# The opening of a two-stage Fourier and MLP kernel in another order: weight rounding, the first weight products, one row turned on TensorE, and the loads

## The chip, the cores and the metric

The kernel runs on one core of a Trainium2 chip. A core has five engines with queues of their own: TensorE (PE, and PEld for its weight loads), VectorE (DVE), ScalarE (ACT), GpSimd (POOL) and SyncE (SP), which only issues transfers here; 16 DMA engines carry them out. An engine takes its instructions in the order in which they were written, and waits at one whose inputs or buffers are not ready. The metric is the device time of one execution in microseconds (us); the median of several runs counts.

## What is computed

```python
def _attn_setup():
    batch, seq, dim = (8, 3008, 256)
...
def _attn_ref(x) -> np.ndarray:
    X = np.fft.fft(x, axis=1)
    X = np.fft.fft(X, axis=2)
    return X.real.astype(np.float32)
...
def _moe_ref(x, w_in, w_out) -> np.ndarray:
    h = x @ w_in
    g = h * (1.0 / (1.0 + np.exp(-1.702 * h)))
    return (g @ w_out).astype(np.float32)
```

The real part of a two-dimensional Fourier transform of each of 8 batches (3008 x 256) goes, row by row, through a layer of width 2048 with a GELU. `x` is float32; the two weight matrices arrive as 64-bit words (`w_in` 256 x 2048, `w_out` 2048 x 256) and are float32 in value after rounding.

## The kernel before

**Stages.** The transform along the sequence has a first stage of length 47 and a second of length 64; the transform along the 256 columns is folded into `w_in`. The first stage (`fold1`, `mix1`; for the first batch `fold_first`, `mix_first`) leaves its result in `xt`. `spill` writes it to a buffer in device memory (`Td`), `fill` reads it back turned (`t4`, 12 blocks). `rotate` rewrites one column of `t4` by a product, and `stage2` makes a tile `pq` from four blocks: 64 small products into two PSUM banks, and four VectorE transposes out of them (L320), two for each bank.

**The main loop** (L669) has 8 batches x 3 blocks x 2 halves x 8 pairs of feature groups: 384 steps and 3 to drain. Step t does `hidden(t)` (TensorE products `pa` and `pb` with the folded weights `wcs`, L448, and a ScalarE copy `v`, L452), `product(t - 3)` (products with `wo`, L515), `activate(t - 1)` (GELU, L477), sums on GpSimd and VectorE, and `rows(t)` on VectorE: L462, then `dif` (L465), which needs the row `nb` and a column of `af2`, then L472. Whatever else belongs to a step hangs in `extra[t]` and is issued at its end, in the order in which it was put there; `early` names the steps at which `fold_w` runs.

**Weights.** Each matrix comes in four chunks (in0 to in3, out0 to out3), 1 MB each, into three buffers `raw`. A chunk goes through
- `bounds`: the square `g` of the high words (ScalarE L359, for in0 VectorE L357), `m`, the high words held within bounds (GpSimd L360), and `r`, the low words as rounding bits, by two ScalarE activations (L362, L363);
- `rounded`: three VectorE instructions, L373 (`m` from `g` and `m`), L375 and L376 (`a` from `m`);
- `finish`: GpSimd adds `a` and `r` (L380), into `wst` for an in-chunk and in two halves into `wo` for an out-chunk.

There is one buffer for `m` and one for `a`, so `m` of a chunk waits for L376 of the chunk before, and L375 of a chunk waits for the chunk before's L380. There are two buffers for `r`.

`fold_w(n)` multiplies `wst[n]` by the column transform (`psw`, L418), copies both halves to `wcs` on ScalarE (L420), and makes a row on one partition (L424). A transfer (L425) turns that row into four columns of `af2`. `hidden(0)` and `hidden(1)` need chunk 0, `hidden(2)` and `hidden(3)` chunk 1, and so on.

**The opening.** Four rounds k of `fold_first` and `mix_first` work on x as it arrives. Each ends in ScalarE copies, of one column in the middle (L248) and into `xt` at the end (L264), and from k = 1 on in a spill, by SP's queue and partly by ScalarE's. The spill of k = 3 goes in two pieces, with the fill of the first four blocks between them. Then come `load_out(0)`, the rounding of in0, five warm-up products (L278), the bounds of in1, `fold_w(0)`, the fill's rest, `load_out(1)`, `rotate`, `stage2`, the rounding of in1, the bounds of out0 and `load_in(2)`. `nyquist(0, 0)` in step 0 makes the row `nb` by a product (`psn`, L331) and a ScalarE copy (L332).

**Buffers that set the order.** Four PSUM banks serve all of `psw`, `psr`, `ps2`, `psn`, `pa` and `pb`: a product that starts a new tile waits until one of the four is read out. All transfers on SP's queue are issued in order; one that waits for its buffer, or for a spill to land, holds those behind it.

Of the kernel before, what the change touches and what calls it, by code (L numbers as in the profile page):

```python
# [27 lines left out]
F32 = mybir.dt.float32  # L28
U32 = mybir.dt.uint32
ALU = mybir.AluOpType  # L30
ACTF = mybir.ActivationFunctionType
# [8 lines left out]
NU, NG = 2, 12  # L40
# [10 lines left out]
def free(ap, offset, *dims):  # L51
    return bass.AP(ap.tensor, ap.offset + offset, [list(ap.ap[0])] + [list(d) for d in dims])
# [57 lines left out]
def kernel(ctx: ExitStack, tc, x, w_in, w_out, tab1, tab2, out):  # L110
    nc = tc.nc
# [14 lines left out]
    cv = ctx.enter_context(tc.tile_pool(name="cv", bufs=1, space=SB))  # L126
# [16 lines left out]
    af2 = const.tile([128, NF], F32, tag="af2", name="af2")  # L143
    ones = const.tile([1, 128], F32, tag="ones", name="ones")
# [5 lines left out]
    def bank(name):  # L150
        return psm.tile([128, 512], F32, tag="mm", name=name)
# [122 lines left out]
    def warm(n):  # L274

        ps = bank("warm")
        for _ in range(n):
            nc.tensor.matmul(ps[:], lhsT=wcs[0][:, 0:128], rhs=wcs[0][:, 0:512], start=True, stop=True)  # L278
# [13 lines left out]
    def fill(b, a0=0, a1=NG):  # L292
        if a0 == 0:
            t4t[b] = tp.tile([128, NG, D], F32, tag="t4", name="t4")
        nc.sync.dma_start(out=t4t[b][:, a0:a1, :], in_=Td[b].rearrange("(a p) d -> p a d", p=128)[:, a0:a1, :])

    def rotate(b, a0=0, a1=NG, copy=None):

        col = t4t[b][:, a0:a1, H]
        ps = bank("psr")  # L300
        nc.tensor.matmul(ps[:, 0:a1 - a0], lhsT=rot, rhs=col, start=True, stop=True)
        (copy or nc.vector.tensor_copy)(col, ps[:, 0:a1 - a0])

    def stage2(b, blk):

        pq, t4 = pqp.tile([128, 2, 512], F32, tag="pq", name="pq"), t4t[b]
        pqt[b, blk] = pq
        ps = [bank("ps2") for _ in range(NU)]
        for cs in range(2):
            for h in range(2):  # L310
                for g in range(4):
                    for u in range(NU):
                        rows, at = slice(64 * u, 64 * u + 64), cs * 256 + h * 128
                        nc.tensor.matmul(ps[u][32 * g:32 * g + 32, at:at + 128], lhsT=m2[rows, cs, h * RUN:(h + 1) * RUN],  # L314
                                         rhs=t4[rows, 4 * blk:4 * blk + 4, cs * H + 32 * g:cs * H + 32 * g + 32],
                                         start=True, stop=True)
        for u in range(NU):
            for cs in range(2):

                nc.vector.transpose(free(pq[:], cs * 512 + u * RUN, [256, 2], [NU * RUN, 4], [1, RUN]),  # L320
                                    free(ps[u][:], cs * 256, [128, 2], [32, 4], [1, 32]))
# [13 lines left out]
    raw = {}  # L335

    def load_in(n, eng):
        t = raw["in", n] = cv.tile([128, 1024, 2], U32, tag="raw", bufs=3, name="raw")
        eng.dma_start(out=t[:].rearrange("p (i f) w -> p i (f w)", i=2),
                      in_=w_in[:, n * 512:(n + 1) * 512].bitcast(U32).rearrange("(i p) f -> p i f", p=128))  # L340

    def load_out(n, eng):
        t = raw["out", n] = cv.tile([128, 1024, 2], U32, tag="raw", bufs=3, name="raw")
        eng.dma_start(out=t[:].rearrange("p (f n) w -> p f (n w)", f=4),
                      in_=w_out[4 * n * 128:(4 * n + 4) * 128, :].bitcast(U32).rearrange("(p f) n -> p f n", p=128))

    pre = {}

    def bounds(key, first=False):


        hi, lo = raw[key][:, :, 1].bitcast(F32), raw[key][:, :, 0]
        g = sp.tile([128, 1024], F32, tag="s", bufs=3, name="g")
        m = cv.tile([128, 1024], F32, tag="m", name="m")
        r = cv.tile([128, 1024], U32, tag="r", bufs=2, name="r")
        if first:
            nc.vector.tensor_tensor(g[:], hi, hi, op=ALU.mult)  # L357
        else:
            nc.scalar.activation(g[:], hi, ACTF.Square)  # L359
        nc.gpsimd.tensor_scalar(m[:], hi, scalar1=TOP, scalar2=-TOP, op0=ALU.min, op1=ALU.max)  # L360

        nc.scalar.activation(r[:].bitcast(F32), lo, ACTF.Copy, scale=2.0 ** -29, bias=2.0 ** 23)  # L362
        nc.scalar.activation(r[:], r[:].bitcast(F32), ACTF.Copy, bias=-2.0 ** 23)  # L363
        pre[key] = g, m, r

    def rounded(outs, key):

# [19 lines left out]
    def round_in(n):  # L387
        wst[n] = op.tile([128, 2, 512], F32, tag="os", name="wst")
        out = wst[n][:].rearrange("p i f -> p (i f)")
        last["in", n] = rounded(lambda *ins: [(out, ins)], ("in", n))  # L390
# [10 lines left out]
    def finish_in(n):  # L401
        last["in", n]()
# [11 lines left out]
    def fold_w(n):  # L414
        for cs in range(2):
            ps = bank("psw")
            for i in range(2):
                nc.tensor.matmul(ps[:], lhsT=cd[:, i, cs, :], rhs=wst[n][:, i, :], start=(i == 0), stop=(i == 1))  # L418

            nc.scalar.copy(wcs[cs][:, n * 512:(n + 1) * 512].rearrange("p (f c) -> p f c", f=4),  # L420
                           free(ps[:], 0, [1, 4], [4, 128]))

        row = cv.tile([1, 512], F32, tag="e", name="row")
        nc.scalar.activation(row[:], ps[0:1, :], ACTF.Copy, scale=2.0)  # L424
        nc.scalar.dma_start(out=af2[:, 4 * n:4 * n + 4], in_=row[:])  # L425


    NP = NF // 2
# [153 lines left out]
    first = tp.tile([128, NG, D], F32, tag="t4", name="first")  # L582
# [16 lines left out]
    for k, need in enumerate(((0, 7, 1), (6, 2), (5, 3), (4,))):  # L599
# [3 lines left out]
        if k:  # L603

            for m in ((0, NM),) if k < 3 else ((0, 16), (16, NM)):
                spill(0, ((0, 2), (2, 1), (3, 1))[k - 1], (nc.sync, nc.scalar if k > 1 else nc.sync), *m)
                if k == 3 and m[0] == 0:
                    fill(0, 0, 4)
    load_out(0, nc.sync)
    bounds(("in", 0), True)  # L610
    round_in(0)
    finish_in(0)
    warm(5)
    bounds(("in", 1))
    fold_w(0)
    fill(0, 4, NG)
    load_out(1, nc.sync)
    rotate(0, 0, 4, nc.scalar.copy)
    stage2(0, 0)
    round_in(1)  # L620
    finish_in(1)
    bounds(("out", 0))
    load_in(2, nc.sync)

    extra, early = {}, {}

    def at(t, fn, *args):
        extra.setdefault(t, []).append((fn, args))

    n = len(steps)  # L630

    ahead = [("out", 0), ("in", 2), ("out", 1), ("in", 3), ("out", 2), ("out", 3)]
    for t, (kind, c) in enumerate(ahead):
# [1 line left out]
        if t + 1 < len(ahead):  # L635
            at(t, bounds, ahead[t + 1])
        at(t + 1, finish_out if kind == "out" else finish_in, c)
    early[1], early[3], early[5] = 1, 2, 3
    for t, load, c in ((0, load_in, 3), (1, load_out, 2), (2, load_out, 3)):
        at(t, load, c, nc.sync)  # L640
    at(3, load_matrices)
    if B > 1:
# [5 lines left out]
    for b in range(B):  # L648
        t0 = b * NBLK * NF
        late = 0 if b else 3  # L650
        if b + 2 < B:
            at(t0 + 10, turn, b + 2)
        if b + 1 < B:
            for c in range(NCH):
                at(t0 + 7 + 2 * c + late, fold1, b + 1, c, nc.gpsimd)
                if c % 2:
                    at(t0 + 8 + 2 * c + late, mix1, b + 1, c // 2)
            at(t0 + 24 + late, spill, b + 1)
            at(t0 + 29 + late, fill, b + 1)
            if b + 2 < B:  # L660
                at(t0 + 33 + late, load_x, b + 2)
            at(t0 + 36 + late, rotate, b + 1)
        for blk in range(NBLK):
            nxt = (b, blk + 1) if blk + 1 < NBLK else (b + 1, 0)
            if nxt[0] < B:
                at(t0 + blk * NF + 8, stage2, *nxt)
                at(t0 + blk * NF + 12, nyquist, *nxt)

    for t in range(n + LAG):  # L669
        if t < n:  # L670
            hidden(t)
        if t == 0:
            nyquist(0, 0)
        if t >= LAG:
            product(t - LAG)
        if t in early:
            fold_w(early[t])

        if 0 < t <= n:
            activate(t - 1)  # L680
            sums(t - 1, nc.gpsimd)
        sums(t - 2, nc.vector)
        if t < n:
            rows(t)
        if t >= LAG:
            combine(t - LAG)
        for fn, args in extra.get(t, ()):
            fn(*args)
# [28 lines left out]
```

## Time and profile before

| | us |
|---|---|
| median of 4 runs | 1934.71 |
| lowest and highest of them | 1933.09 to 1935.99 |
| the profiled execution, its own time | 1932.98 |
| its span | 1931.0 |
| PE busy in the span | 1905.1 (99%) |
| DVE, ACT, POOL busy | 1408.1, 673.5, 764.6 |

The span runs from the first to the last instruction of the profiled execution; its time has 1.98 us more around it. Busy time counts an engine's instructions, without branches, waits and the issuing of transfers. A matmul in float32 is recorded as two passes, so a `psw` group of four matmuls is "x8". A wait's bracket, "[1.17 <-POOL wo L380]", names the idle time of the engine just before that row and whose instruction ended it. The chain that ended last is followed back from the last instruction; in it, "DMA raw" is time from the issue of a transfer to its landing.

### The profile page before, as it was taken

Reading aid. Unit: us, or ns where it says so; the run is one execution under the profiler, and the core shown is the slowest. Engines: PE = TensorE matmul, PEld = TensorE weight load, DVE = VectorE, ACT = ScalarE, POOL = GpSimd, SP = SyncE. Lnnn points to the kernel's source line nnn. Section 1 sums busy time; section 2 is a strip of 40 time slices with the busy share of each in tenths; the row PEclk is TensorE's granted clock in tenths of the full one; section 3 lists DMA queues with packets and bytes.
Section 4 is the critical chain, followed back from the end, with each engine's and each line's share of the span. In section 5 each row is a group of like instructions: output and inputs, shape, how many; then the busy total and the mean of one; then the engine's idle time right before and its main releaser. Section 6 shows DMA issues by size and latency. Waiting matters only on the chain.

```text
span 1931.0 us, 29514 instructions
## 1 busy us (share of the span) xinstructions
PE 1905.1 (99%) x10822; PEld 1667.1 (86%) x10822; DVE 1408.1 (73%) x2924; ACT 673.5 (35%) x928; POOL 764.6 (40%) x1061
## 2 busy tenths in 40 slices
PE   7899999999999999999999999999999999999998
PEld 4698888988889888888889888898888988889887
DVE  4777777876778767876777777777777777777766
ACT  4633333333333333333333333333333333333332
POOL 3665323542245322552235523364323642223222
PEclk9999999999999999999999999999999999999999
DMA  8730550227203452126322262221820223202201
GB/s 286 173 53 10 109 65 12 51 55 112 17 12 59 65 93 17 25 46 106 52 27 49 40 101 39 18 49 43 121 20 13 18 48 56 17 12 27 17 12 22
DMA packets 145552, 104.54 MB, mean 54 GB/s; under 512 B 105474, under 2 KB 128290, under 8 KB 143712
## 3 DMA queue, kind: packets, MB, share of 16 engines
q1 hardware_dynamic: 142976, 99.07, 30.4%
q0 software_dynamic: 384, 2.10, 0.4%
q8 instruction: 86, 1.41, 0.3%
q10 hardware_dynamic: 2048, 1.48, 0.3%
q14 instruction: 58, 0.48, 0.1%
HBM read 59.36 MB, written 48.01 MB: 56 GB/s over the span
## 4 chain that ended last, share of the span: by engine, by line
PE 96%; DMA 2%; ACT 1%; DVE 0%; POOL 0%; issue 0%; SPq 0%; ACTq 0%; DVEq 0%; POOLq 0%
PE po L515 59%; PE pa L448 17%; PE pb L448 17%; PE ps L210 1%; PE ps L314 1%; DMA xt<-in_x_dram 1%; DMA raw<-in_moe_w_in_dram 1%; PE psw L418 0%; DMA Td<-xt 0%; DMA af<-row 0%; PE ps L214 0%; POOL xt L229 0%; PE ps L259 0%; DVE e L237 0%; ACT g L359 0%
## 5 line engine op out<-in xcount | busy, mean ns | idle before, releaser
L489 POOL TENSOR_TENSOR s<-h 128x256 f32<-128x256 f32 (+1 forms) x376 | 270.3, 719 | 1093.6 <-ACT h L477 1028.0
L515 PE MATMUL po<-s,wt 128*128 128x256 f32 (+1 forms) x2256 | 599.7, 375 | 0.0
L452 ACT COPY v<-pa 128x512 f32<-128x512 f32 (+1 forms) x384 | 222.0, 578 | 1062.6 <-PE pa L448 1062.6
L462 DVE TENSOR_TENSOR h<-v,pb 128x512 f32<-128x512 f32 (+1 forms) x384 | 259.0, 674 | 402.8 <-PE pb L448 396.7
L515 PEld LDWEIGHTS po<-s,wt 128*128 128x128 f32 x2256 | 428.6, 190 | 48.4
L515 PE MATMUL po<-h,wo 128*128 128x256 f32 (+1 forms) x1632 | 469.7, 375 | 0.1
L477 ACT ACTIVATE h<-h 128x1024 f32<-128x1024 f32 (+1 forms) x384 | 400.8, 1044 | 18.2 <-DVE h L472 15.3
L448 PE MATMUL pa<-pq,wcs 128*128 128x256 f32 (+1 forms) x1536 | 393.8, 379 | 2.2 <-DVE pq L320 1.3
L448 PE MATMUL pb<-pq,wcs 128*128 128x256 f32 (+1 forms) x1536 | 387.9, 375 | 1.8 <-DVE dif L465 1.6
L515 PEld LDWEIGHTS po<-h,wo 128*128 128x128 f32 x1632 | 310.0, 190 | 36.0 <-issue 0.5
L448 PEld LDWEIGHTS pa<-pq,wcs 128*128 128x128 f32 x1536 | 286.8, 190 | 51.1 <-issue 11.9
L465 DVE SCALAR_TENSOR_TENSOR dif<-nb,af,pb 128x256 f32<-128x256 f32 (+1 forms) x768 | 328.2, 468 | 1.9 <-DMA af<-row 1.9
L448 PEld LDWEIGHTS pb<-pq,wcs 128*128 128x128 f32 x1536 | 291.5, 190 | 35.9 <-DVE dif L465 2.0
L490 POOL TENSOR_TENSOR s<-h 128x256 f32<-128x256 f32 (+1 forms) x376 | 276.7, 736 | 0.0
L472 DVE TENSOR_TENSOR h<-pa,dif 128x512 f32<-128x512 f32 (+1 forms) x448 | 265.4, 604 | 13.2
L515 PE MATMUL po<-h,wt 128*128 128x256 f32 (+1 forms) x752 | 220.3, 375 | 0.0
L515 PE MATMUL po<-s,wo 128*128 128x256 f32 (+1 forms) x752 | 220.3, 375 | 0.0
L493 DVE TENSOR_TENSOR s<-h,s 128x256 f32<-128x256 f32 (+1 forms) x376 | 204.0, 543 | 12.9
L492 DVE TENSOR_TENSOR s<-s,h 128x256 f32<-128x256 f32 (+1 forms) x376 | 178.8, 476 | 4.3 <-POOL s L489 4.3
L515 PEld LDWEIGHTS po<-h,wt 128*128 128x128 f32 x752 | 142.9, 190 | 16.1
L515 PEld LDWEIGHTS po<-s,wo 128*128 128x128 f32 x752 | 142.9, 190 | 16.1
L196 POOL TENSOR_TENSOR xt<-xt 111x510 f32<-111x510 f32 x56 | 73.8, 1318 | 4.4
(67 smaller groups left out, 699.8 us busy)
## 6 DMA issues: line engine op xcount, KB each, us to landing
out_dram<-os SPq DMA_DIRECT2D x284, 64.0 KB
Td<-xt SPq DMA_DIRECT2D x14, 768.0 KB
t<-Td SPq DMA_DIRECT2D x7, 1536.0 KB
xt<-in_x_dram SPq DMA_DIRECT2D x14, 512.0 KB
xt<-Xr SPq DMA_DIRECT2D x14, 512.0 KB
nb<-pq SPq DMA_DIRECT2D x23, 256.0 KB
out_dram<-os SPq DMA_DIRECT2D x96, 56.0 KB
Xr<-in_x_dram SPq DMA_DIRECT2D x7, 752.0 KB
```

The costliest lines, as they stand in the source:

```text
L196: eng.tensor_tensor(low, low, free(t, up + D - 1, [-D, 2], [-1, D - 1]), op=ALU.add)
L448: nc.tensor.matmul(ps[:, i * 256:i * 256 + n], lhsT=wcs[cs][:, f * 128:(f + 1) * 128], rhs=pq[:, cs, ks], start=True, stop=True)
L452: nc.scalar.copy(two(v[:], n), two(pa[:], n))
L462: nc.vector.tensor_tensor(two(h[:], n), two(v[:], n), two(pb[:], n), op=ALU.add)
L465: nc.vector.scalar_tensor_tensor(dif[:, i * 256:i * 256 + n], nb[:, ks], af2[:, f:f + 1], pb[:, i * 256:i * 256 + n], op0=ALU.mult, op1=AL ...
L472: nc.vector.tensor_tensor(free(h[:], 512 + at + m - 1, [256, 2], [RUN, blocks], [-1, m]), *ins, op=ALU.add)
L477: nc.scalar.activation(g, g, ACTF.Gelu_apprx_sigmoid)
L489: eng.tensor_tensor(s1, a21, a22, op=ALU.add)
L490: eng.tensor_tensor(s3, a11, a21, op=ALU.subtract)
L492: eng.tensor_tensor(s2, s1, a11, op=ALU.subtract)
L493: eng.tensor_tensor(s4, a12, s2, op=ALU.subtract)
L515: nc.tensor.matmul(pot[q][:, i, :n], lhsT=lhs, rhs=rhs, start=(p == 0 and i == 0 and f == 0), stop=(p == NP - 1), skip_group_check=True)
```

## The change

- `stage2` issues the four transposes in another order: first the `cs = 0` half of both banks, then the `cs = 1` half.
- The two activations that make `r` are a function `low_bits`. For in0 they run in the opening right after round k = 1, and `bounds` takes their result; for the other chunks they run inside `bounds` as before.
- `fold_w(0)` turns its row into the columns of `af2` by four products (L424's row as weights, one column of ones), and a ScalarE copy; the other three chunks keep the transfer.
- In the opening, `load_in(2)` follows `load_out(0)`; in1 is rounded and finished ahead of `fold_w(0)`; four warm-up products, not five, stand after that; the copy in `rotate` is VectorE's and not ScalarE's.
- `fold_w(1)` moves from step 1 to step 0. `load_out(1)` moves to step 0, the fill's rest and `load_in(3)` to step 1, `load_out(2)` and `load_out(3)` to steps 2 and 3.

```diff
-        for u in range(NU):
-            for cs in range(2):
+        for cs in range(2):
+            for u in range(NU):
 
                 nc.vector.transpose(free(pq[:], cs * 512 + u * RUN, [256, 2], [NU * RUN, 4], [1, RUN]),
                                     free(ps[u][:], cs * 256, [128, 2], [32, 4], [1, 32]))
...
-    def bounds(key, first=False):
-
-
-        hi, lo = raw[key][:, :, 1].bitcast(F32), raw[key][:, :, 0]
+    def low_bits(key):
+        r = cv.tile([128, 1024], U32, tag="r", bufs=2, name="r")
+
+        nc.scalar.activation(r[:].bitcast(F32), raw[key][:, :, 0], ACTF.Copy, scale=2.0 ** -29, bias=2.0 ** 23)
+        nc.scalar.activation(r[:], r[:].bitcast(F32), ACTF.Copy, bias=-2.0 ** 23)
+        return r
+
+    def bounds(key, r=None):
+
+
+        hi = raw[key][:, :, 1].bitcast(F32)
         g = sp.tile([128, 1024], F32, tag="s", bufs=3, name="g")
         m = cv.tile([128, 1024], F32, tag="m", name="m")
-        r = cv.tile([128, 1024], U32, tag="r", bufs=2, name="r")
-        if first:
+        if r:
             nc.vector.tensor_tensor(g[:], hi, hi, op=ALU.mult)
         else:
             nc.scalar.activation(g[:], hi, ACTF.Square)
         nc.gpsimd.tensor_scalar(m[:], hi, scalar1=TOP, scalar2=-TOP, op0=ALU.min, op1=ALU.max)
-
-        nc.scalar.activation(r[:].bitcast(F32), lo, ACTF.Copy, scale=2.0 ** -29, bias=2.0 ** 23)
-        nc.scalar.activation(r[:], r[:].bitcast(F32), ACTF.Copy, bias=-2.0 ** 23)
-        pre[key] = g, m, r
+        pre[key] = g, m, r or low_bits(key)
...
-        nc.scalar.dma_start(out=af2[:, 4 * n:4 * n + 4], in_=row[:])
+        if n:
+            nc.scalar.dma_start(out=af2[:, 4 * n:4 * n + 4], in_=row[:])
+            return
+        ps = bank("psf")
+        for f in range(4):
+            nc.tensor.matmul(ps[:, f:f + 1], lhsT=free(row[:], f, [4, 128]), rhs=ones[:, 0:1], start=True, stop=True)
+        nc.scalar.copy(af2[:, 0:4], ps[:, 0:4])
...
                 if k == 3 and m[0] == 0:
                     fill(0, 0, 4)
-    load_out(0, nc.sync)
-    bounds(("in", 0), True)
+        if k == 1:
+            r0 = low_bits(("in", 0))
+    for load, c in ((load_out, 0), (load_in, 2)):
+        load(c, nc.sync)
+    bounds(("in", 0), r0)
     round_in(0)
     finish_in(0)
-    warm(5)
     bounds(("in", 1))
-    fold_w(0)
-    fill(0, 4, NG)
-    load_out(1, nc.sync)
-    rotate(0, 0, 4, nc.scalar.copy)
-    stage2(0, 0)
     round_in(1)
     finish_in(1)
+    warm(4)
+    fold_w(0)
+    rotate(0, 0, 4)
+    stage2(0, 0)
     bounds(("out", 0))
-    load_in(2, nc.sync)
...
-    early[1], early[3], early[5] = 1, 2, 3
-    for t, load, c in ((0, load_in, 3), (1, load_out, 2), (2, load_out, 3)):
+    early[0], early[3], early[5] = 1, 2, 3
+    at(0, load_out, 1, nc.sync)
+    at(1, fill, 0, 4, NG)
+    for t, load, c in ((1, load_in, 3), (2, load_out, 2), (3, load_out, 3)):
         at(t, load, c, nc.sync)
```

## The prediction

> **What bounds the kernel now.** I first read the windows view in three stretches, then the waits and the chain of waits of the opening, then the timeline row by row. The columns of a windows row are start:end, length, then the busy time and count of PE, PEld, DVE, ACT and POOL, then PE clock, DMA share and GB/s.
>
> ```profile
> 0.00:80.00 80.00, 60.72 (x460) 37.47 (x461) 45.11 (x63) 46.04 (x64) 33.98 (x35) 0.94 0.81 252
> 80.00:1900.00 1820.00, 1820.00 (x10252) 1608.49 (x10251) 1347.03 (x2830) 621.37 (x858) 724.07 (x1017) 1.00 0.30 46
> 1900.00:1931.00 31.00, 24.41 (x114) 21.14 (x112) 16.01 (x33) 6.06 (x8) 6.58 (x10) 0.97 0.08 18
> ```
>
> From 80 to 1900 us TensorE is never idle. The change adds almost no TensorE work there and takes none away, so its whole effect is the moment at which TensorE becomes continuously busy. Before 80 it stands still for 19.28 us in all, and much of that is the wait for x. So I follow only the opening, and ask when product 2 starts (79.01 in the chain below), after which TensorE has no gap.
>
> ```profile
> POOL wst L380 <- DVE a L376: 10.1, 1, 10.1
> POOL wst L380 <- ACT r L363: 8.4, 1, 8.4
> ACT g L359 <- DMA raw<-in_moe_w_in_dram: 2.8, 1, 2.8
> ```
>
> These waits (us, times, longest) are the ones that the change goes for: chunk in0 waits for ScalarE's low bits, chunk in1 for VectorE, and ScalarE's Square for the late load of chunk in2. The chain of waits (start, length) shows which of them reach the end:
>
> ```profile
> 33.27 4.03 DMA Td<-xt
> ...
> 38.46 11.52 DMA raw<-in_moe_w_in_dram
> ...
> 50.06 1.15 ACT g L359
> ...
> 64.10 5.41 PE psw L418 x8
> ...
> 70.63 6.30 DMA af<-row
> 76.95 0.88 DVE dif L465 x2
> ...
> 79.01 3.45 PE po L515 x16
> 82.46 3.43 PE psw L418 x8
> ```
>
> The load of in2 sits in SP's queue behind a fill that waits for the spill, lands at 50.02 and sends ScalarE late into its work. The timeline gives the rest; the bracket is the idle time before a row and what ended it:
>
> ```profile
> 33.54 2.36 POOL L380 TENSOR_TENSOR wst<-a,r 128x1024 uint32<-128x1024 uint32 x1 [8.40 <-ACT r L363]
> 42.41 1.44 DVE L320 STREAM_TRANSPOSE pq<-ps 128x256 f32<-128x256 f32 x4 [11.67 <-PE ps L314]
> 45.50 0.29 PEld L331 LDWEIGHTS psn<-pq,ones 1*128 1x128 f32 x2 [0.33 <-issue]
> 58.50 0.69 DVE L375 TENSOR_SCALAR a<-m 128x1024 uint32<-128x1024 uint32 x1 [1.17 <-POOL wo L380]
> 66.00:68.00 2.00, 2.00 (x3) 0.67 (x2) 1.97 (x3) 1.30 (x3) 0.66 (x1) 0.50 1.15 211
> ```
>
> The fourth row shows a second limit: VectorE's rounding of a chunk waits until GpSimd has added the chunk before. The last (a windows row again) is a TensorE clock of half for some 4 us, of which more below.
>
> **The change, step by step.** Durations are rows of this trace.
>
> *Low bits of in0 early.* ScalarE ends its copies of k=1 at 24.43 and next ran at 24.98. Two activations (31.23 to 33.46, 2.23 us) now come in between, so the L248 copies of k=2 start at 26.66: 1.68 later, and with them the second half of mix_first 2, all of k=3 and the spills that ScalarE's own queue issues. TensorE ends mix_first 3 at 30.9 (29.2), the last xt copy ends at 32.0 (30.31), fill 0:4 is issued at 34.55 (32.85). In return the GpSimd add of in0 waits only for VectorE (29.52+1.23): 30.8 to 33.15, where it ended at 35.90.
>
> *Warm 4, then fold_w(0).* Four warm products are 8 passes of 0.43, 3.44 us: 30.9 to 34.3. That covers the wait until 33.15; without them fold_w(0) would start 1.1 earlier. It runs 34.3 to 37.75 instead of 35.95 to 39.4: a gain of 1.65.
>
> *The row by products.* Before, copies and row ended 1.35 after psw (40.75), then an issue of 0.56, and the rotation's copy stood behind it on ScalarE (41.44). Now the row ends at 39.1 and four products, 8 passes, follow on TensorE, with rotate and stage 2 queued behind them. No row shows a product of one column. From below: the two weight loads of the psn row, 0.18 each, take 0.29 together, so they start 0.11 apart; 8 x 0.11 = 0.9. From above: a pass of the main products, 3.45/16 = 0.215, so 1.7. The operands are nearest to psn's (one row), so I take 1.0: 40.15. Rotation 0.35, its copy on an idle VectorE under stage 2's first half, two halves of 0.67 each: 41.85. The transposes start at 41.95; in the new order pa needs two (0.36 each) and not three: pa 0 at 42.75 (43.58), a gain of 0.83. The 1.65 is half lost, to the round trip row, TensorE. In the later 23 blocks the transposed tile is read 8 steps on, so the order is worth nothing there. The row's transfer, which held dif 0 until 48.69, is gone; dif 0 now waits for nb, at 46.4.
>
> *Loads.* On SP: out0 at 35.5, in2 at 36, out1 after ScalarE's last read of in1 (36.5), the fill's rest at about 39, in3 at 45.5. In2 has 1.5 MB ahead of it and not 3.5, so I put it at 44, from 50.02; it is wanted at 51 (below), and out0 (landed by 41.49, at most 7.7 after issue, so by 43.2) delays v 0 by at most 1.5, which has 2 us of slack at fold_w(1)'s copies. Fill 0:4 landed no later than 39.06, 6.2 after issue: now by 40.75, 0.6 late at worst. The fill's rest is read at 75; out2, out3, tables and x of batch 1 follow about 1 us earlier, for readers 50 us away: nothing.
>
> *fold_w(1) at step 0.* Its chunk is ready at about 40 (49.45). TensorE: pa, pb and psn take 2.97 as before, to 45.7; then fold_w(1) to 49.15, where TensorE had waited. But on ScalarE its two copies, row and issue (49.45 to 51.06) now stand ahead of in2's three activations, with v 1 behind both: 51.06+3.21 = 54.3, where v 1 ran at 53.27. That eats the early landing. v 1 ends at 54.87; rows(1) on VectorE takes 2.2 (53.86 to 56.06 before): 57.1; then the rounding of in2, 1.22+0.69+1.23 with gaps: 60.4. Before: 59.23+1.23 = 60.46. There GpSimd's add of out0 held L375 by 1.17; now that add ends at 56.0, and v 1 is late instead. GpSimd then takes m of out1 and the add of in2 (1.1+2.36 with the waits between): psw 2 can start at 64.05, and started at 64.10.
>
> Sum of the steps: **-0.1 us**. The rest of the way (psw 2, row, its transfer, dif 4, product 2) is unchanged.
>
> *The clock.* TensorE stood idle from 61.99 to 64.10; psw 2 then took 5.41 where psw 3, the same eight passes, takes 3.43 (from 82.46), at a granted clock of 0.50: 1.97 us, all on the chain. Yet the gap of 2.2 us ahead of psw 0 (33.74 to 35.95) cost no clock. So a gap of this size sometimes costs 2 us and sometimes none. After the change there is a longer gap: hidden 2 ends at 52.5, hidden 3 needs the banks that rows(1) frees (56.5). If the half clock falls behind that one, product 0 (3.45, ready at 58.2) ends at 61.7 to 64, still ahead of psw 2, fills the later gap, and psw 2 runs at full clock: -1.97. If not, nothing changes: 0. I take the middle, -1.0; a new half-clock stretch on stage 2 and pa 0 would be +1.97.
>
> [...]
>
> **Forecast.** The profiled execution took 1932.98 us (span 1931.0 and 1.98 around it), the median of the four runs is 1934.71, 1.73 above it. 1932.98-1.1 = 1931.9; as a median 1931.9+1.73 = 1933.6.
>
> **Rivals.** *Faster.* If v 1 is not late (in2's activations run under fold_w(1) by ScalarE starting sooner, or the row's products at 0.9), the next limit for L375 is GpSimd's add at 56.0 and not 58.5: -2.5, and with the half clock gone -1.97: 1934.71-4.5 = **1930.2**. For it: the chunk in1 is done 9 us sooner and TensorE has work ready. Against it: ScalarE has no idle time from 49.4 to v 1.
>
> *Slower.* Fill 0:4 lands late. Three transfers, some 2.3 MB (the spill's rest, out0, in2), now follow it at once; if they share the 16 DMA engines with it, it takes 5 us more, rotate starts at 45.7, and since every step to psw 2 is tight, psw 2 starts 4.9 late: **1939.6**. It decides from a landing at about 44.5 on (0.2% is 3.9 us). Against it: before, the 1 MB of out0 was issued 0.97 us behind the fill as well, and it had landed by 39.06.
>
> *It doesn't do what it says.* If load in2 still waits (its buffer is in0's, free only after VectorE's g, 27.4, so it should not), ScalarE stalls until 50 as before, where fold_w(1) holds it until 51 anyway: 1934.6, no different.
>
> **How the numbers follow.** About 0.2% (3.9 us) is what a measurement of this kernel can tell from no change. No change: 0.62, time 1933.6, its own range 1932.5 (products 0.9, clock -1.97 and not -1.0) to 1937.9 (products 1.7, fill 0.6 late, clock +1.97). Faster 0.26 at 1930.2, slower 0.12 at 1939.6. A few hundredths of the first case's tail go to faster: 0.28, 0.60, 0.12. The range reaches down to the faster case, 1929.5, and up to the end of the own range, 1937.9; it leaves out the slower case and a little of the faster.
>
> **What would show it.** Right: GpSimd's first add near 30.8, psw 0 near 34.3 with no gap after warm, about 1.0 us of small products behind a gap of 1.3, pa 0 near 42.8, L376 of in2 ending near 60.4, psw 2 near 64. Wrong: v 1 before 53, L376 of in2 before 59, or rotate waiting for a transfer; or TensorE with gaps after 80.

## The result, and the profile after

| | kernel before | changed kernel |
|---|---|---|
| median of the runs, us | 1934.24 (52 runs) | 1937.38 (34 runs) |
| lowest to highest, us | 1931.82 to 1937.89 | 1934.16 to 1940.08 |
| ratio, 95% interval | | 1.0013 (1.0008 to 1.0018) |
| profiled execution, its span, us | 1932.98, 1931.0 | 1935.38, 1933.2 |

The change makes the kernel slower by 0.13%: some 2.5 us (1.5 to 3.5; the two medians lie 3.1 apart, within that). The runs of one kernel scatter over 6 us, more than the change is worth, so only medians over many runs and their interval carry a verdict; a single profile shows where time goes, with the clock as it was granted in that one execution.

The windows view (columns as before) says at once that nothing happened behind the opening:

```profile
0.00:80.00 80.00, 60.68 (x456) 39.88 (x456) 43.82 (x61) 43.82 (x61) 31.76 (x35) 0.85 0.78 241
80.00:1900.00 1820.00, 1819.97 (x10250) 1608.47 (x10251) 1346.19 (x2827) 622.53 (x859) 724.71 (x1017) 1.00 0.30 46
```

TensorE is as full as before from 80 on. It is also as *busy* ahead of 80 (60.68 against 60.72 us), but the granted clock there is 0.85 and not 0.94, so part of that busy time is the same work done at the clock of 0.50 that the two-microsecond windows below show. The chain of waits, which ran through transfers and ScalarE before, now runs through TensorE. The line numbers are the changed kernel's: L433 are the four products of the row, L421 the old L418, L457 `pa` and `pb`, L524 `product`. A number behind a name is the step or the chunk: pa 0 and v 1 belong to `hidden(0)` and `hidden(1)`, product 2 is `product(2)`, psw 1 are the products of `fold_w(1)`.

```profile
31.40 3.63 PE warm L278 x8
35.03 3.45 PE psw L421 x8
39.62 2.02 PE psf L433 x8
41.96 2.00 PE ps L314 x64
44.87 2.04 PE pa L457 x4
46.91 1.71 PE pb L457 x4
48.62 1.15 PE psn L331 x2
...
55.17 1.15 ACT g L365
...
68.54 3.45 PE psw L421 x8
...
81.16 3.45 PE po L524 x16
```

Product 2 starts at 81.16 and not at 79.01: 2.15 us, the whole difference of the spans. Psw 2 starts 4.4 later (68.54 against 64.10 in the two chains) and gets 2 back by running at full clock. The timeline (start, length, bracket as before) and the clock in the two-microsecond windows:

```profile
32.23 2.36 POOL L383 TENSOR_TENSOR wst<-a,r 128x1024 uint32<-128x1024 uint32 x1 [5.75 <-DVE a L379]
39.62 2.02 PE L433 MATMUL psf<-ones,row 1*128 1x1 f32 x8 [1.15 <-ACT row L427]
43.94 1.44 DVE L320 STREAM_TRANSPOSE pq<-ps 128x256 f32<-128x256 f32 x4 [1.77 <-PE ps L314]
58.94 0.69 DVE L471 TENSOR_TENSOR h<-v,pb 128x512 f32<-128x512 f32 x1 [3.82 <-ACT v L461]
...
40.00:42.00 2.00, 2.00 (x18) 1.97 (x25) 0.00 (x1) 0.16 (x1) 1.42 (x1) 0.98 1.00 416
42.00:44.00 2.00, 1.85 (x64) 1.39 (x64) 0.23 (x2) 1.92 (x2) 1.15 (x1) 0.50 1.06 436
44.00:46.00 2.00, 1.13 (x3) 0.98 (x4) 1.38 (x4) 1.32 (x2) 0.00 (x0) 0.50 0.99 411
46.00:48.00 2.00, 2.00 (x7) 1.54 (x5) 0.00 (x0) 0.58 (x1) 0.00 (x0) 0.50 1.03 351
```

GpSimd's add of in0 no longer waits for ScalarE, as meant. Then TensorE stands for 1.15 us until the row is made, spends 2.02 us on four products of one column, and the granted clock falls to 0.50: stage 2, pa 0 and pb 0 all run at it. The fourth row is the end of it: VectorE waits 3.82 us for v 1.

### The profile page after: what moved, and what is told of

The parts are those of the page before. It is cut to its first block, busy times and chain, and to the rows that moved or that the text cites. A ratio compares the mean times of both kernels' runs of the same rounds, so it can differ in the third digit from the quotient of the medians.

```text
span 1933.2 us, 29524 instructions
## 1 busy us (share of the span) xinstructions
PE 1907.2 (99%) x10828; PEld 1671.4 (86%) x10828; DVE 1408.2 (73%) x2925; ACT 673.5 (35%) x928; POOL 763.5 (39%) x1061
## 4 chain that ended last, share of the span: by engine, by line
PE 97%; ACT 1%; DVE 1%; issue 0%; ACTq 0%
PE po L524 59%; PE pa L457 17%; PE pb L457 17%; PE ps L314 1%; PE ps L210 1%; PE psw L421 1%; PE ps L214 0%; PE warm L278 0%; DVE dif L474 0%; ACT r L352 0%; ACT g L365 0%; ACT r L353 0%; PE psf L433 0%; DVE os L541 0%; DVE h L471 0%
## 5 line engine op out<-in xcount | busy, mean ns | idle before, releaser
L524 PE MATMUL po<-s,wt 128*128 128x256 f32 (+1 forms) x2256 | 599.6, 375 | 0.0
L524 PE MATMUL po<-h,wo 128*128 128x256 f32 (+1 forms) x1632 | 470.5, 376 | 0.0
L524 PEld LDWEIGHTS po<-s,wt 128*128 128x128 f32 x2256 | 428.6, 190 | 48.4
L457 PE MATMUL pa<-pq,wcs 128*128 128x256 f32 (+1 forms) x1536 | 395.6, 380 | 4.7 <-DVE dif L474 3.6
L457 PE MATMUL pb<-pq,wcs 128*128 128x256 f32 (+1 forms) x1536 | 389.6, 376 | 1.5 <-DVE dif L474 1.2
L524 PEld LDWEIGHTS po<-h,wo 128*128 128x128 f32 x1632 | 310.9, 190 | 35.9
L457 PEld LDWEIGHTS pa<-pq,wcs 128*128 128x128 f32 x1536 | 287.8, 191 | 53.0 <-issue 11.1
L457 PEld LDWEIGHTS pb<-pq,wcs 128*128 128x128 f32 x1536 | 292.8, 191 | 36.0 <-DVE dif L474 1.6
L524 PE MATMUL po<-h,wt 128*128 128x256 f32 (+1 forms) x752 | 220.3, 375 | 0.0
L524 PE MATMUL po<-s,wo 128*128 128x256 f32 (+1 forms) x752 | 220.3, 375 | 0.0
L524 PEld LDWEIGHTS po<-h,wt 128*128 128x128 f32 x752 | 142.9, 190 | 16.1
L524 PEld LDWEIGHTS po<-s,wo 128*128 128x128 f32 x752 | 142.9, 190 | 16.1
```

The lines of the kernel that those rows point to most:

```text
L457: nc.tensor.matmul(ps[:, i * 256:i * 256 + n], lhsT=wcs[cs][:, f * 128:(f + 1) * 128], rhs=pq[:, cs, ks], start=True, stop=True)
L524: nc.tensor.matmul(pot[q][:, i, :n], lhsT=lhs, rhs=rhs, start=(p == 0 and i == 0 and f == 0), stop=(p == NP - 1), skip_group_check=True)
```

## The experiments

My theory after these profiles: the row's round trip (TensorE waits for ScalarE, then does tiny products, with rotate and stage 2 behind them in its queue) costs more than all the other edits gain. Rivals: ScalarE's order, with chunk in2's activations behind fold_w(1)'s copies; and the early low bits, which delay x, the spill and the fill. Every ratio is to the kernel before, run on the same chip.

**e1: the row by transfer again**

```diff
-        if n:
+        if True:
             nc.scalar.dma_start(out=af2[:, 4 * n:4 * n + 4], in_=row[:])
             return
```

> The changed kernel with one part undone: the row of chunk 0 goes into af2 by a transfer again, not by four products. Theory (the row's round trip on TensorE is the loss): rotate follows psw 0 at once at about 38.5 us, pa 0 starts near 41.5 instead of 44.87, TensorE keeps its full clock from 42 to 49, psw 1 starts near 45 instead of 49.68, and the ratio to the kernel before falls from 1.0013 to 0.9995 to 1.0000. Rival (ScalarE's order: chunk in2's activations behind fold_w(1)'s row): v 1 stays late whatever TensorE does, ratio 1.0008 to 1.0013. Rival (the early low bits delay x, the spill and the fill): nothing changes, 1.0013.

Measured: 0.9985 (0.9977 to 0.9994), median 1931.70. Its TensorE in the timeline:

```profile
40.16 0.36 PE L301 MATMUL psr<-t,small 128*128 128x4 f32 x2 [0.84 <-DMA t<-Td]
40.44 1.16 PE L314 MATMUL ps<-t,small 64*32 64x128 f32 x64
42.48 1.13 PE L457 MATMUL pa<-pq,wcs 128*128 128x256 f32 x4 [0.88 <-DVE pq L320]
...
45.45 3.70 PE L421 MATMUL psw<-wst,small 128*128 128x512 f32 x8
```

Without this one part, the change is a gain of 0.15%. From psw 0's end to pa 0 it takes 3.2 us and not 6.4; psw 1 starts at 45.45, not 49.68, and the clock stays at 1.00 from 40 to 48. v 1 runs at 54.08, not 58.34: ScalarE's lateness was TensorE's, handed on. The theory holds, and the gain is larger than it expected. Rotate now waits for the fill (to 40.16), which the products had covered.

**e5: the products alone, in the kernel before**

```diff
-        nc.scalar.dma_start(out=af2[:, 4 * n:4 * n + 4], in_=row[:])
+        if n:
+            nc.scalar.dma_start(out=af2[:, 4 * n:4 * n + 4], in_=row[:])
+            return
+        ps = bank("psf")
+        for f in range(4):
+            nc.tensor.matmul(ps[:, f:f + 1], lhsT=free(row[:], f, [4, 128]), rhs=ones[:, 0:1], start=True, stop=True)
+        nc.scalar.copy(af2[:, 0:4], ps[:, 0:4])
```

> The kernel before with one part of the change alone: the row of chunk 0 by four products, right behind fold_w(0), and nothing else. Theory (row's round trip on TensorE, 2.0 us of products and 1.2 of waiting): rotate and stage 2 start some 2 us later, pa 0 near 45 to 46 instead of 43.58, and the clock may fall to half there; but the late landing of in2 at 50 hides part of it: ratio 1.0003 to 1.0015. Rival (what costs is the order of ScalarE and the loads, not the products): dif 0 is 1.2 us sooner, ratio 0.9995 to 1.0000.

Measured: 1.0024 (1.0015 to 1.0033), median 1938.84. The part alone costs 4.6 us (0.0024 x 1934.5), more than I expected; taking it out of the changed kernel gains 5.4 (1.0013 less 0.9985). Two runs from opposite sides agree on the cause within their intervals. The profile of e5 holds one loss more that is not the products':

```profile
38.14 5.40 PE L418 MATMUL psw<-wst,small 128*128 128x512 f32 x8 [2.22 <-POOL wst L380]
...
49.32 2.08 PE L454 MATMUL pa<-pq,wcs 128*128 128x256 f32 x4 [1.20 <-DVE pq L320]
```

Psw 0 ran at half clock behind a gap of 2.22 us. The kernel before has that gap as well, and in its profile it cost no clock. The half clock of pa 0 (2.08 us) comes behind the products.

**e2: the products' weights packed.** How much of it is the length of the products? Their weights were every fourth value of the row; here ScalarE writes the row in the order of its columns.

```diff
+            nc.scalar.activation(row[:].rearrange("p (f c) -> p f c", f=4), free(ps[0:1, :], 0, [1, 4], [4, 128]), ACTF.Copy, scale=2.0)
...
-            nc.tensor.matmul(ps[:, f:f + 1], lhsT=free(row[:], f, [4, 128]), rhs=ones[:, 0:1], start=True, stop=True)
+            nc.tensor.matmul(ps[:, f:f + 1], lhsT=row[:, f * 128:(f + 1) * 128], rhs=ones[:, 0:1], start=True, stop=True)
```

> The changed kernel with the row written in the order of its columns, so that the four products' weights are 128 neighbouring values and not every fourth one; same products, same sums. If the prediction's price of the products was only mis-sized by the stride of their weights: eight passes take about 0.9 us instead of 2.02 and pa 0 starts 1.1 us earlier; with the half clock still there the ratio is 1.0007, with the half clock gone 0.9998. If the length of a pass has nothing to do with the stride: 2.0 us again, ratio 1.0013.

Measured: 1.0004 (0.9995 to 1.0012). The rows by source line, of the changed kernel and then of this one (ns, least, median and most); the added lines shift the numbers, and L436 here is L433, L460 is L457:

```profile
L433 PEld LDWEIGHTS psf<-ones,row x8: 304/324/327, 39.6 to 41.2; 1*128 1x128 f32 x8
```

```profile
L436 PEld LDWEIGHTS psf<-ones,row x8: 181/187/187, 40.9 to 41.7; 1*128 1x128 f32 x8
40.88 1.05 PE L436 MATMUL psf<-ones,row 1*128 1x1 f32 x8 [1.15 <-ACT row L430]
44.30 2.05 PE L460 MATMUL pa<-pq,wcs 128*128 128x256 f32 x4 [0.97 <-DVE pq L320]
```

A strided weight load took 0.324 us here, a packed one 0.187, and the eight passes 1.05 and not 2.02. The ratio falls with it (by 0.0009, 1.7 us), but the intervals overlap, from 1.0008 to 1.0012: the size rests on the rows. The half clock at pa 0 (2.05 us) is still there.

**e7: the same, with TensorE kept busy in both gaps**

```diff
+        warm(1)
         ps = bank("psf")
...
     stage2(0, 0)
+    warm(1)
     bounds(("out", 0))
```

> The changed kernel with packed weights (e2), and one warm-up product in each of the two gaps on TensorE: while the row is made, and while VectorE transposes. Nothing on the chain gets longer by more than 0.1 us. Theory (half the loss of e2 is the clock): pa 0, pb 0 and psn run at full clock, 1.5 to 2 us are saved, ratio 0.9993 to 0.9998. Rival (the clock's loss lies under another wait): as e2, 1.0004.

Measured: 0.9990 (0.9981 to 0.9999).

```profile
41.56 0.39 PE L301 MATMUL psr<-t,small 128*128 128x4 f32 x2
41.87 1.16 PE L314 MATMUL ps<-t,small 64*32 64x128 f32 x64
42.96 1.12 PE L278 MATMUL warm<-wcs 128*128 128x512 f32 x2
43.92 1.11 PE L461 MATMUL pa<-pq,wcs 128*128 128x256 f32 x4
```

Two products whose results nobody reads save 0.14% (2.7 us by the ratios, whose intervals overlap from 0.9995 to 0.9999; the two profiles show 1.5 of it up to psw 1): pa 0 takes 1.11 us, and psw 1 starts 11.05 after psw 0 and not 12.57. So the second half of the loss is the clock, and it lies on the chain.

**e3: fold_w(1) back at step 1**, with the row as in the changed kernel

```diff
-    early[0], early[3], early[5] = 1, 2, 3
+    early[1], early[3], early[5] = 1, 2, 3
```

> The changed kernel with fold_w(1) back at step 1. Theory (row's round trip): pa 0 and the half clock stay as they are, v 1 comes sooner but fold_w(1) later, ratio 1.0008 to 1.0018. Rival (ScalarE's order): in2's activations start near 50.4 and not 55.2, v 1 at 53.7 instead of 58.34, rounding of in2 ends 3 us or so earlier, ratio 0.9995 to 1.0000.

Measured: 1.0000 (0.9991 to 1.0009). The rival has a share: v 1 ran at 54.33, as it said, not at 58.34. But VectorE's L379 of in2 ended only 1.65 earlier, at 62.68, since it then waited for GpSimd. So the loss of the changed kernel is the row's products together with the early `fold_w(1)`: undoing either takes it away (the products e1, the step this run). One thing more in its timeline bears on the clock, and is taken up at the end of the next section:

```profile
40.45 2.02 PE L433 MATMUL psf<-ones,row 1*128 1x1 f32 x8 [1.15 <-ACT row L427]
42.40 0.39 PE L301 MATMUL psr<-t,small 128*128 128x4 f32 x2
42.72 1.24 PE L314 MATMUL ps<-t,small 64*32 64x128 f32 x64
```

**e8: the same move with the row by transfer**

```diff
-        if n:
+        if True:
...
-    early[0], early[3], early[5] = 1, 2, 3
+    early[1], early[3], early[5] = 1, 2, 3
```

> The changed kernel with the row by transfer (e1) and fold_w(1) back at step 1. If fold_w(1) at step 0 costs by ScalarE's order alone (v 1 behind in2's activations behind the row): v 1 near 50.5 instead of 54.1, ratio 0.9970 to 0.9980. If with the row out of the way GpSimd's add of out0 sets the pace of the rounding: no gain, ratio 0.9983 to 0.9990.

Measured: 0.9991 (0.9982 to 1.0000); e1 had 0.9985. v 1 ran at 49.87, four us before e1's, and nothing came of it:

```profile
58.93 0.69 DVE L378 TENSOR_SCALAR a<-m 128x1024 uint32<-128x1024 uint32 x1 [1.16 <-POOL wo L383]
```

With the row off TensorE, GpSimd's add of out0 sets the pace of the rounding, as in the kernel before. In this profile psw 1 also ran at half clock (5.37 us, behind a gap of 2.51), so the ratio, and not this trace, says what the move is worth. As far as e3 and e8 show, the step of fold_w(1) counts only while TensorE is late.

**e4: the low bits of in0 late again**

```diff
-        if k == 1:
-            r0 = low_bits(("in", 0))
...
+    r0 = low_bits(("in", 0))
     bounds(("in", 0), r0)
```

> The changed kernel with the low bits of in0 made after round k = 3 again. Theory (row's round trip): mix_first ends 1.7 us earlier, but GpSimd's add of in0 starts near 33.5 instead of 32.2 and psw 0 near 35.9 instead of 34.9: 1 us later, ratio 1.0015 to 1.0020. Rival (early low bits): the spill and fill 1.7 us earlier are what counts, ratio 1.0004 or below.

Measured: 1.0026 (1.0015 to 1.0038), worse than both outcomes I had written down, though its interval takes in the first, and against the second rival.

```profile
37.07 5.40 PE L421 MATMUL psw<-wst,small 128*128 128x512 f32 x8 [3.08 <-POOL wst L383]
```

The early low bits are a gain of some 2.5 us (0.0013; the intervals meet between 1.0015 and 1.0018), in spite of the 1.7 that they cost x. Part of it is the clock: without them TensorE idles for 3.08 us ahead of psw 0, and psw 0 and psw 2 both take 5.40.

**e6: packed products behind nyquist, ahead of fold_w(1)**

```diff
+        turned_row.append(row)
+
+    turned_row = []
+
+    def turn_row():
+        row = turned_row.pop()
         ps = bank("psf")
...
             nyquist(0, 0)
+            turn_row()
```

> The changed kernel with packed weights (e2) and the four products issued behind nyquist in step 0, ahead of fold_w(1), so that rotate and stage 2 don't stand behind the row. Theory (place, not length): the products still take 1.05 us, but pa 0 starts near 42.5 with full clock, psw 1 near 46.5 to 47; ratio 0.9980 to 0.9992, near the transfer's 0.9985. Rival (any such products on TensorE ahead of fold_w(1) cost their length and the clock): as e2, 1.0000 to 1.0006.

Measured: 0.9997 (0.9988 to 1.0006), a miss.

```profile
45.84 0.94 PE L442 MATMUL psf<-ones,row 1*128 1x1 f32 x8
47.68 5.37 PE L421 MATMUL psw<-wst,small 128*128 128x512 f32 x8 [0.90 <-ACT af L443]
```

I had overlooked the fourth PSUM bank: `pa`, `pb`, `psn` and the products hold all four, so psw 1 waits 0.90 until ScalarE has read one out, and then runs at half clock. Place matters, but this place has a wait of its own.

**e9: packed products behind stage 2**, in the gap in which TensorE waits for the transposes

```diff
     stage2(0, 0)
+    turn_row()
     bounds(("out", 0))
```

> The changed kernel with packed weights, and the four products issued behind stage 2, in the gap of 0.9 us in which TensorE waits for VectorE's transposes. Theory (place and not length): rotate and stage 2 don't wait for the row, the products' 0.95 us lie in a gap, dif 0 has its columns by 43 and not at 49.5 as with the transfer: pa 0 near 42.6, psw 1 near 45.6, ratio 0.9978 to 0.9987. Rival (small products on TensorE cost the clock wherever they stand): half clock from pa 0 on, ratio 0.9993 to 1.0002.

Measured: 0.9986 (0.9977 to 0.9995).

```profile
39.57 1.16 PE L314 MATMUL ps<-t,small 64*32 64x128 f32 x64
40.65 1.05 PE L442 MATMUL psf<-ones,row 1*128 1x1 f32 x8
41.63 1.13 PE L466 MATMUL pa<-pq,wcs 128*128 128x256 f32 x4
...
53.88 0.69 DVE L480 TENSOR_TENSOR h<-v,pb 128x512 f32<-128x512 f32 x1 [2.82 <-ACT v L470]
```

The same four products give a ratio 0.0018 lower here than ahead of rotate (e2). They are as good as the transfer, no better: `dif 0` has its columns 3 us sooner than in e1 (46.35 against 49.55), but then VectorE waits 2.82 for v 1 instead.

**e10 and e11: v ahead of the next chunk's activations on ScalarE**, on top of e9 and of e1

```diff
-            at(t, bounds, ahead[t + 1])
+            mid[t + 1] = ahead[t + 1]
...
             hidden(t)
+        if t in mid:
+            bounds(mid[t])
```

> As e9, and the next chunk's square and low bits stand behind the next step's v on ScalarE, not ahead of it. If ScalarE's order is the second limit: v 1 near 51 instead of 54, rounding of in2 done near 58.7 instead of 61, psw 2 near 62.3 instead of 64.7, ratio 0.9965 to 0.9980. If GpSimd's adds set the pace of the rounding whatever ScalarE does: as e9 within 0.0005.

> As e1 (row by transfer), with v ahead of the next chunk's activations. The row lands at 49.5, so the rounding of out0 ends near 54.3 as in e1 and only 0.4 us of v 1's lateness can be saved there: ratio 0.9980 to 0.9987. If ScalarE's order counts in the later steps too: 0.9970 to 0.9980.

Measured: e10 0.9970 (0.9960 to 0.9981), median 1928.51; e11 0.9981 (0.9972 to 0.9989), median 1930.46. The timeline of e10:

```profile
50.42 0.59 ACT L470 COPY v<-pa 128x512 f32<-128x512 f32 x1 [0.62 <-PE pb L466]
51.36 0.68 DVE L480 TENSOR_TENSOR h<-v,pb 128x512 f32<-128x512 f32 x1
56.16 0.69 DVE L378 TENSOR_SCALAR a<-m 128x1024 uint32<-128x1024 uint32 x1 [1.17 <-POOL wo L383]
61.73 3.70 PE L421 MATMUL psw<-wst,small 128*128 128x512 f32 x8 [1.34 <-POOL wst L383]
```

v 1 is out of the way at 51, the rounding of in2 follows GpSimd at once, and psw 2 starts at 61.73, at full clock. The granted clock of this trace is 1.00 from 30 to 80, the only one of the thirteen in which it doesn't fall there; what that alone is worth was not separated. e10 beats the kernel before by 0.30% and the changed kernel by 0.43% (8.3 us by the ratios). e11, whose row still comes by transfer, stays 2 us behind in the median (the intervals overlap from 0.9972 to 0.9981); e9 and e1, without this edit, differ by less than their intervals. So, as far as these intervals carry, the products in the gap pay only once v is out of the way.

## Why the prediction was wrong

It forecast no change, 1933.6, slightly faster; the kernel became slower, by less than the 0.2% that it had set as the bound. Step by step:

- **What bounds, and where to look**: right. TensorE is full from 80 on, and 2.15 us at product 2 are the 2.2 us of the spans.
- **Low bits early**: right in kind. The add of in0 started at 32.23; the 1.4 us over the predicted 30.8 are x, whose last pieces VectorE could fold only from 23.00 on in this execution (21.65 in the one before). That moment differs from execution to execution: with the same opening, the last 32 products of mix_first 3 start at 30.25 here, at 31.10 in e1 and at 31.51 in e2. e4 shows that the part is a gain.
- **Warm 4, fold_w(0)**: right; psw 0 follows warm with no gap, at 34.9 (predicted 34.3, the rest being x).
- **The row by products: the step that failed.** It said "8 x 0.11 = 0.9" from below and 1.7 from above, "I take 1.0". They took 2.02, above both bounds: the bounds came from rows with packed weights, and the weights of these products are strided. A row exists for that difference only in e2's run, whose packed products took 1.05: the estimate held for the weights that it was made from. The wait of 1.15 ahead of them was right (1.3).
- **The clock: the other half of the failure.** It named a half-clock stretch on stage 2 and pa 0, at "+1.97", but only as an end of the range. It took -1.0, looking only at the later gap, where the half clock can lie under a wait. Both happened: 42 to 48 at 0.50 in the chain (stage 2 2.00 for 1.3, pa 0 to psn 4.8 for 2.97), and later hidden 3 and the start of product 0 at half clock (60.47 to 65.8), with psw 2 at 3.45. The second spell is not wholly under a wait: GpSimd's add of in2 was done at 67.87, and product 0 held TensorE until psw 2 started at 68.37, another 0.5. Not -1.0 but some +2.5, +0.5 and -2.
- **fold_w(1) at step 0 and v 1**: right in mechanism. It had v 1 at 54.3 by ScalarE's order; e1, with the row off TensorE, measured 54.08. In the changed kernel everything from pa 0 on was 4 us later (v 1 58.34).
- **Loads**: right. In2 was never waited for; the slow rival (the fill late) did not happen: it landed by 40.16 in e1, within the 40.75 given.
- **Rotate, transposes**: the copy on VectorE ran at once (42.00), pa 0 followed two transposes and not three.

Put together: the products 1.0 dearer, x 0.6 later and the half clock's 2.5 make 4.1 us, and psw 1 started 4.0 later than predicted (49.68 against 45.7). GpSimd's add of in2 handed on 3.8 of them, product 0 added its 0.5, and psw 2 started 4.3 late (68.37 against 64.05); its full clock gives 2 back. The rest of the change is worth a gain of 0.15% (e1). The granted clock fell to 0.50 at 41.9, behind a gap of 1.15 us and 2.02 us of one-column products, which the trace counts as busy, and ahead of the second gap (43.85 to 44.87).

**When the clock falls.** The prediction had to leave open why a gap of some 2 us costs 2 us in one place and nothing in another. In the changed kernel the granted clock was 0.50 from 41.9 to 48.7 and from 59.0 to 65.8 (windows of 0.2 us). Rows of seven traces, set beside each other:

| trace, row | TensorE idle ahead, us | one-column products ahead, us | the row took, us |
|---|---|---|---|
| before, psw 0 | 2.21 | none | 3.70 |
| before, psw 2 | 2.10 | none | 5.41 |
| e4, pa of hidden 3 | 3.62 | none | 1.13 |
| e4, psw 2 | 2.03 | none | 5.40 |
| changed, stage 2 | 1.15 | 2.02 | 1.96 |
| e2, pa 0 | 1.15 and 0.97 | 1.05 | 2.05 |
| e3, pa 0 | 1.15 and 0.93 | 2.02 | 2.05 |
| e7, pa 0 | 0.29 | 1.05 | 1.11 |
| e9, pa 0 | 0.94 | 1.05 | 1.13 |

At a granted clock of 1.00 psw 1 took 3.70, stage 2 1.16 and pa 0 1.13 (e1). The length of a gap alone does not sort the rows: in e4 pa of hidden 3 took 1.13 behind 3.62 us, and psw 2 took 5.40 behind 2.03. Where one-column products stood ahead, the clock fell in the changed kernel, in e2 and in e3, and held in e7 and e9, with 0.29 and 0.94 us of idle time beside them. Whether such products count for the clock as idle time does, and what else decides, was not shown. So these traces do not tell beforehand whether a single gap of 2 us costs anything.

## What to carry to other kernels

A wait taken off one engine by giving a little work to the engine that bounds was dear here (4.6 us in e5): the work itself (2.02 us), the round trip that the bounding engine now waits for (1.15), and everything in its queue behind both. Put such work where that engine waits anyway (the 0.9 us of transposes held four products), count PSUM banks there (a wait of 0.90 in e6), and keep weights packed (1.05 us and not 2.02 in e2). Where TensorE has gaps of a microsecond and tiny products close together, look at the granted clock of the windows behind them before costing anything; in e7 a full-size product in each of two gaps, of 1.15 and 0.97 us in e2, saved 2.7 us by the ratios.

## What the runs showed of the hardware

- A weight load of 1x128 with every fourth value took 0.324 us (changed kernel), a packed one 0.187 (e2); eight such passes took 2.02 and 1.05.
- The granted clock fell to 0.50 for 6.8 us behind a gap of 1.15 us and 2.02 us of one-column products (changed kernel, 41.9 to 48.7). With packed products and one warm product in each of the two gaps it was 1.00 from 40 to 48 (e7); with packed products alone it was 0.50 from 44 to 46 (e2). In the kernel before, a gap of 2.2 us cost no clock (psw 0 took 3.70) and one of 2.1 us cost 1.97 us (psw 2 took 5.41); why was not shown.
- A transfer of one row of 2 KB into four columns, issued at 40.45 while the DMA engines were 0.99 to 1.06 busy (windows from 40 to 48), was waited for until 49.55 (e1).
